# Block attention and two expert layers on one core: keys of the first block stored once and cut into windows by the matmul, with a new hand-written start order

## The chip, the cores and the metric

The program runs on one core of a Trainium2 chip. The metric is device time in microseconds (us) of one execution. The engines named here are TensorE (PE, with its weight loads shown apart as PEld), VectorE (DVE), ScalarE (ACT), GpSimd (POOL) and the queue that issues the transfers (SP). Each engine works through its own list in order and waits where an operand is not ready.

## The reference

Three layers follow each other on 4 x 768 tokens with 8 heads of 64 dimensions. The first is attention in chunks of 32 queries: each chunk sees 8 memory keys, 16 keys to its left, its own 32 and 8 to its right, so 64 keys in all.

```
for c in range(nc):                      # chunks of 32
    k_ctx = k[:, :, max(0, 32c-16) : min(S, 32c+40)]
    k_full = concat([mem_k, k_ctx])      # 8 + 56 keys
    a = softmax(q_c @ k_full.T / 8)
    out[:, :, chunk c] = a @ v_full
x = out as (3072 tokens, 512)
x = (s * relu(x @ w_in)**2 + b) @ w_out              # 512 -> 2048 -> 512
logits = x @ phi; slots = softmax over tokens of logits, transposed, @ x
slot_out = relu(slots @ w1[e]) @ w2[e]               # 8 experts, 4 slots each
result = softmax over slots of logits, @ slot_out
```

## The kernel before

The 3072 tokens are six blocks of 512 (16 chunks). A unit `u` of attention is one block and one pair of heads, so a block has four units; units 0 to 3 are the first block. For a unit, `Q[u % 2]` holds the queries of 16 chunks spread so that the two heads of a chunk stand in 64 columns, with zeros where the other head's dimensions are. The keys lie in memory as 16 windows of 64 (8 memory keys and 56 of context), overlapping ones written out twice, and `load_k` brings all of a unit, 512 KB, in one transfer. `att_qk` (L198) makes 16 products, one a chunk: 64 weight columns (the queries) against 64 moving columns (the window). An fp32 product is two instructions in the trace, so a unit shows 32. Even and odd pairs of chunks write the upper and lower 64 partitions of a bank.

Then `att_exp` takes the maximum over each window (L212), subtracts it (L213) and lets ACT exponentiate (L214). `att_norm` sums (L218), adds a tiny number (L219), inverts (L220), and POOL multiplies (L221). `att_tr` transposes on PE (L227) and copies the result into `PB[u % 2]` in two halves: the first on ACT (L236), the second on ACT (L238, argument `fast`) or on DVE (L240). `att_pv` multiplies with the values (L247) and ACT and DVE split the result into a high and a low part (L251, L263).

The second layer's weights come as halves of a packed form in seven staging slots (`w_load`). A half is decoded by `w_begin` (L293 on DVE, L294 and L295 on ACT) and `w_end` (L301 on DVE). `wi_high` (L312) and `wi_low` (L316) split a decoded half. `mm_h` (L332) and `mm_job` (L353) are the large products of the second layer, which follow for the rest of the kernel.

The first block's order is a string written by hand, `START`. Each token is a step and the number is its unit: `q`, `k`, `v`, `w`, `c` issue transfers (queries, keys, values, a weight half, the constants), `z` runs warming products on PE (L927), `S` spreads the queries (L184 on ACT, L185 on POOL or DVE), `A` is `att_qk`, `m` `att_exp`, `n` `att_norm`, `T` `att_tr`, `P` `att_pv`, `x` the low part, `D` and `E` the decoding, `I` and `i` the split of a weight, `H` a quarter of the first `mm_h`. The string fixes the order on every engine and queue; after it a scheduler mixes in the DVE and ACT work of the next steps. Eight transfers can be under way, and the ninth is issued when the first has landed.

Of the kernel before, what the change touches and what calls it, by code (L numbers as in the profile page):

```python
# [15 lines left out]
P = 128  # L16
NB = 6
NF = 16
NHP = 4
CB = 16  # L20
# [3 lines left out]
NEG = -3.0e38  # L24
EPS = 1e-9
START = (
# [3 lines left out]
)  # L30
# [8 lines left out]
def tile_attention_moe_softmoe(  # L39
    ctx: ExitStack,  # L40
    tc: tile.TileContext,
    q0d: bass.AP,
    qd: bass.AP,
    kd: bass.AP,
# [104 lines left out]
    def qv(u):  # L149
        return Q[u % 2].rearrange("p (c h n) -> p c h n", h=2, c=CB)  # L150
# [4 lines left out]
    def kv(u):  # L155
        t = K[u] if u < 2 else (Y[u - 2] if u < 4 else K[u % 2])
        return t.rearrange("p (c n) -> p c n", c=CB)

# [19 lines left out]
    def load_k(u):  # L178
        j, hp = jh(u)
        sp.dma_start(out=kv(u), in_=kd[j, hp].rearrange("p (c n) -> p c n", c=CB))  # L180

# [9 lines left out]
    def att_qk(u, b):  # L191
        S = b.rearrange("p (t n) -> p t n", t=8)
        qt, kt = qv(u), kv(u)
        for i in range(4):
            for z in range(2):
                for par in range(2):
                    c = 4 * i + 2 * par + z
                    pe.matmul(S[64 * par:64 * par + 64, 2 * i + z, :], lhsT=qt[:, c].rearrange("p h n -> p (h n)"), rhs=kt[:, c, :],  # L198
                              start=True, stop=True)

# [712 lines left out]
    with tc.manual_schedule(engines={mybir.EngineType.PE, mybir.EngineType.SP}):  # L913
# [30 lines left out]
        def s_pv(u):  # L944
# [4 lines left out]
        steps = {  # L949
            "c": lambda _: sp.dma_start(out=cons, in_=cd),  # L950
            "q": load_q,
# [7 lines left out]
            "n": lambda u: att_norm(u, pool),  # L959
            "T": lambda u: att_tr(u, sbank(), u < 3),  # L960
            "P": s_pv,
# [278 lines left out]
def _layouts(q, k, v, mem_k, mem_v, moe_w_in, moe_w_out, moe_s, moe_b, moe2_phi, moe2_w1, moe2_w2):  # L1240
# [21 lines left out]
    vw = windows(v, mem_v)  # L1262
    kt = np.ascontiguousarray(kw.transpose(0, 2, 3, 5, 1, 4)).reshape(NB, NHP, P, CB * 64)
    vt = np.ascontiguousarray(
# [15 lines left out]
    for d0, width in PARTS:  # L1280
        per = 1024 // width
        w2.append(moe2_w2[:, :, d0:d0 + width].reshape(2, 4, 8 // per, per, P, width)
                  .transpose(0, 2, 1, 4, 3, 5).reshape(-1, P, 1024))
    return {"q0d": np.ascontiguousarray(qt[0]), "qd": qp, "kd": kt, "vd": vt, "wd": w.view(np.int64), "e1d": np.ascontiguousarray(moe2_w1),
            "e2d": np.concatenate(w2), "cd": c}
# [15 lines left out]
```

## Time and profile before

| what | value |
|---|---|
| median of 3 runs | 672.23 us (671.5 to 672.26) |
| the profiled execution | 673.84 us, of which 672.0 us lie from its first to its last instruction |
| PE busy | 653.4 us, 97% of the span |
| DVE, ACT busy | 397.1 us, 328.3 us |
| TensorE clock granted, mean | 0.993 of full |

Start times in the trace count from the span's first instruction. A busy PE counts a matmul's whole passage, and the passages of neighbours overlap, so the time from one start to the next is shorter than the duration of one.

### The profile page before, as it was taken

Reading aid. Unit: us, or ns where it says so; the run is one execution under the profiler, and the core shown is the slowest. Engines: PE = TensorE matmul, PEld = TensorE weight load, DVE = VectorE, ACT = ScalarE, POOL = GpSimd, SP = SyncE. Lnnn points to the kernel's source line nnn. Section 1 sums busy time; section 2 is a strip of 40 time slices with the busy share of each in tenths; the row PEclk is TensorE's granted clock in tenths of the full one; section 3 lists DMA queues with packets and bytes.
Section 4 is the critical chain, followed back from the end, with each engine's and each line's share of the span. In section 5 each row is a group of like instructions: output and inputs, shape, how many; then the busy total and the mean of one; then the engine's idle time right before and its main releaser. Section 6 shows DMA issues by size and latency. Waiting matters only on the chain.

```text
span 672.0 us, 12487 instructions
## 1 busy us (share of the span) xinstructions
PE 653.4 (97%) x4983; PEld 518.7 (77%) x4983; DVE 397.1 (59%) x707; ACT 328.3 (49%) x592; POOL 123.3 (18%) x118
## 2 busy tenths in 40 slices
PE   7899999999999998999999999999999999999995
PEld 4678888888878887888788887887887888877374
DVE  4799997666774577655576576434444445333333
ACT  4898884554654455444445554233442334233332
POOL 5100000233433585344434100000000000000000
PEclk9999999999999998999999999999999999999999
DMA  8999934476556856788754684256777777999987
GB/s 337 407 398 360 322 115 161 152 224 202 204 176 191 296 206 246 269 297 297 263 209 173 220 305 134 93 180 233 249 258 250 272 248 279 409 362 409 346 328 283
DMA packets 50745, 174.09 MB, mean 259 GB/s; under 512 B 5632, under 2 KB 5632, under 8 KB 50688
## 3 DMA queue, kind: packets, MB, share of 16 engines
q1 hardware_dynamic: 50688, 173.30, 72.0%
q8 instruction: 39, 0.64, 0.4%
q14 instruction: 18, 0.15, 0.1%
HBM read 139.72 MB, written 33.55 MB: 258 GB/s over the span
## 4 chain that ended last, share of the span: by engine, by line
PE 92%; DVE 4%; ACT 2%; issue 1%; DVEq 0%; POOL 0%; ACTq 0%; POOLq 0%
PE bank L353 39%; PE bank L671 22%; PE bank L332 11%; PE bank L247 4%; PE bank L198 4%; PE bank L1163 2%; PE bank L1122 2%; PE bank L227 2%; PE bank L405 2%; PE bank L379 1%; PE bank L421 1%; PE bank L1192 1%; PE bank L927 1%; DVE w L301 0%; ACT sp L295 0%
## 5 line engine op out<-in xcount | busy, mean ns | idle before, releaser
L353 PE MATMUL bank<-g,wo 128*128 128x512 f32 x672 | 165.0, 395 | 0.0
L353 PEld LDWEIGHTS bank<-g,wo 128*128 128x128 f32 x672 | 123.6, 188 | 28.7 <-issue 1.7
L332 PE MATMUL bank<-x,wi 128*128 128x512 f32 x384 | 93.1, 390 | 0.2 <-DVE x L263 0.2
L332 PEld LDWEIGHTS bank<-x,wi 128*128 128x128 f32 x384 | 71.8, 188 | 15.5 <-DVE x L263 0.6
L686 ACT ACTIVATE rt1n<-y1n 128x1024 f32<-128x1024 f32 x16 | 16.9, 1059 | 73.3 <-DVE y1n L797 73.3
L1090 POOL MEMSET x10n<- 128x1024 f32 x1 | 1.0, 957 | 241.1 <-ACT ees L413 241.1
L341 DVE SCALAR_TENSOR_TENSOR rt<-bank,cons,rt 128x512 f32<-128x512 f32 x32 | 23.9, 747 | 33.8 <-ACT rt L336 33.7
L316 POOL TENSOR_TENSOR wi<-w,wi 128x512 fp32r<-128x512 f32 x16 | 20.7, 1292 | 116.9 <-ACT wi L312 110.9
L792 DVE TENSOR_TENSOR y1n<-bank,y1n 128x512 f32<-128x512 f32 x16 | 11.1, 691 | 45.7 <-PE bank L671 45.6
L679 ACT ACTIVATE g<-rt0n,cons 128x512 fp32r<-128x512 f32 x32 | 23.1, 723 | 20.2 <-DVE rt0n L689 20.2
L324 ACT ACTIVATE wo<-w 128x512 fp32r<-128x512 f32 x32 | 20.1, 629 | 24.7 <-PE bank L353 16.0
L325 POOL TENSOR_TENSOR wo<-w,wo 128x512 fp32r<-128x512 f32 x16 | 22.3, 1397 | 50.0 <-ACT wo L324 37.7
L312 ACT ACTIVATE wi<-w 128x512 fp32r<-128x512 f32 x32 | 20.1, 627 | 23.0 <-PE bank L332 21.9
L683 DVE SCALAR_TENSOR_TENSOR g<-rt0n,cons,g 128x512 fp32r<-128x512 f32 x32 | 24.7, 773 | 10.0 <-ACT g L679 9.5
L353 PE MATMUL bank<-g,yt0n 128*128 128x512 f32 x120 | 30.1, 398 | 0.2 <-DVE sp L372 0.2
L353 PE MATMUL bank<-g,yt1n 128*128 128x512 f32 x120 | 29.6, 395 | 0.0
L247 PEld LDWEIGHTS bank<-pb,v 128*64 128x64 f32 x704 | 22.6, 139 | 8.9 <-issue 3.5
L343 DVE SCALAR_TENSOR_TENSOR g<-rt,cons,g 128x512 fp32r<-128x512 f32 x32 | 24.1, 754 | 5.4 <-ACT g L342 4.9
L689 DVE SCALAR_TENSOR_TENSOR rt0n<-bank,cons,rt0n 128x512 f32<-128x512 f32 x16 | 12.0, 750 | 25.8 <-ACT rt0n L686 25.8
L198 PEld LDWEIGHTS bank<-k,q 128*64 128x64 f32 x704 | 23.2, 142 | 5.1 <-issue 4.7
L342 ACT ACTIVATE g<-rt,cons 128x512 fp32r<-128x512 f32 x32 | 23.0, 720 | 7.2 <-DVE rt L341 7.1
L353 PEld LDWEIGHTS bank<-g,yt0n 128*128 128x128 f32 x120 | 21.9, 188 | 5.8 <-DVE sp L372 0.9
(484 smaller groups left out, 1461.2 us busy)
## 6 DMA issues: line engine op xcount, KB each, us to landing
sp<-wd SPq DMA_DIRECT2D x24, 512.0 KB, 9.8
wo<-dws SPq DMA_DIRECT2D x24, 512.0 KB, 4.5
k<-kd SPq DMA_DIRECT2D x22, 512.0 KB, 7.0
v<-vd SPq DMA_DIRECT2D x22, 512.0 KB, 5.3
q<-qd SPq DMA_DIRECT2D x20, 512.0 KB, 6.6
dws<-wo SPq DMA_DIRECT2D x16, 512.0 KB, 6.9
yt0n<-dws SPq DMA_DIRECT2D x12, 512.0 KB, 4.9
yt1n<-dws SPq DMA_DIRECT2D x12, 512.0 KB, 4.2
```

The costliest lines, as they stand in the source:

```text
L198: pe.matmul(S[64 * par:64 * par + 64, 2 * i + z, :], lhsT=qt[:, c].rearrange("p h n -> p (h n)"), rhs=kt[:, c, :], start=True, stop=True)
L247: pe.matmul(b[64 * h:64 * h + 64, 64 * m:64 * m + 64], lhsT=vt[:, m, h, :], rhs=pb[:, m // 2, m % 2, h].rearrange("p z n -> p (z n)"), sta ...
L316: (dve if n < NF else pool).tensor_tensor(out=r32(t[:, 1]), in0=raw, in1=t[:, 0], op=ALU.subtract)
L325: (dve if n < NF else pool).tensor_tensor(out=r32(t[:, 1]), in0=raw, in1=t[:, 0], op=ALU.subtract)
L332: pe.matmul(HB[n % 2], lhsT=r32(w[:, a, kt, :]), rhs=r32(x[:, b]), start=(kt == 0 and i == 0), stop=(kt == 3 and i == 2))
L341: dve.scalar_tensor_tensor(out=t, in0=HB[n % 2], scalar=s_col, in1=r, op0=ALU.mult, op1=ALU.mult)
L342: act.activation(out=r32(g[:, 0]), in_=t, func=AF.Identity, bias=b_col)
L343: dve.scalar_tensor_tensor(out=r32(g[:, 1]), in0=t, scalar=b_col, in1=g[:, 0], op0=ALU.add, op1=ALU.subtract)
L353: pe.matmul(yb[dt], lhsT=r32(w[:, a, dt * 128:dt * 128 + 128]), rhs=r32(g[:, b]), start=(first and i == 0), stop=(last and i == 2))
L671: pe.matmul(b, lhsT=r32(wv[:, a, kt, :]), rhs=r32(xv[:, c]), start=(first and kt == 0 and i == 0), stop=(kt == 1 and i == 2), skip_group_c ...
L679: act.activation(out=r32(hl(dst)[:, 0]), in_=t, func=AF.Identity, bias=b_col)
L683: dve.scalar_tensor_tensor(out=r32(g[:, 1]), in0=t, scalar=b_col, in1=g[:, 0], op0=ALU.add, op1=ALU.subtract)
```

## The change

Keys of the first block are stored once per head pair: `KRAW` = 536 columns (16 empty ones, then the block's 512 positions and the 8 behind it) and the 8 memory keys, so 544 columns, 272 KB where 512 KB were. The windows of a chunk are cut by the matmul: `att_qk` makes two products a chunk for the units 0 to 3, one of 56 moving columns out of the context and one of 8 moving columns out of the memory keys, both with the same queries as weights. Other blocks keep their windows. The constants come in two loads: the identity (128 columns) early, the rest behind `q4`. The first weight half is issued behind `k3`, no longer ahead of the constants. The start order is a new one, and only units 0 and 1 copy both halves of the transposed weights on ACT (before: 0 to 2).

```diff
+KRAW = 16 + 512 + 8
 START = (
-    "q0 k0 q1 k1 w1 c0 q2 k2 v0 q3 k3 v1 w1 v2 w1 v3 w1 "
-    "z2 S0 A0 z1 S1 A1 m0 n0 D0 S2 m1 A2 E0 T0 I0 n1 S3 m2 z1 P0 T1 A3 i0 n2 x0 m3 P1 T2 D1 n3 x1 E1 H0 P2 "
-    "k4 w1 q4 w1 k5 v4 w1 q5 T3 H1 P3 x2 D2 H2 x3 E2 D3 E3 y0 w9 v5"
+    "q0 k0 q1 k1 c0 q2 k2 v0 q3 k3 w1 v1 w1 v2 w1 v3 w1 "
+    "z2 S0 A0 z1 S1 A1 m0 S2 A2 m1 n0 S3 A3 m2 n1 T0 D0 m3 n2 P0 E0 T1 n3 I0 x0 T2 i0 P1 D1 H0 x1 T3 P2 E1 "
+    "k4 w1 q4 c1 w1 k5 v4 w1 q5 x2 H1 P3 D2 H2 x3 E2 D3 E3 y0 w9 v5"
 )
 def load_k(u):
     j, hp = jh(u)
-    sp.dma_start(out=kv(u), in_=kd[j, hp].rearrange("p (c n) -> p c n", c=CB))
+    if j:
+        sp.dma_start(out=kv(u), in_=kd[j - 1, hp].rearrange("p (c n) -> p c n", c=CB))
+    else:
+        sp.dma_start(out=kraw(u), in_=k0d[hp])
 def att_qk(u, b):
...
-                    pe.matmul(S[64 * par:64 * par + 64, 2 * i + z, :], lhsT=qt[:, c].rearrange("p h n -> p (h n)"), rhs=kt[:, c, :],
-                              start=True, stop=True)
+                    dst, q = S[64 * par:64 * par + 64, 2 * i + z, :], qt[:, c].rearrange("p h n -> p (h n)")
+                    if u < NHP:
+                        kt = kraw(u)
+                        pe.matmul(dst[:, 8:64], lhsT=q, rhs=kt[:, 32 * c:32 * c + 56], start=True, stop=True)
+                        pe.matmul(dst[:, 0:8], lhsT=q, rhs=kt[:, KRAW:KRAW + 8], start=True, stop=True)
+                    else:
+                        pe.matmul(dst, lhsT=q, rhs=kv(u)[:, c, :], start=True, stop=True)
 steps = {
-            "c": lambda _: sp.dma_start(out=cons, in_=cd),
+            "c": lambda i: sp.dma_start(out=cons[:, (0, 128)[i]:(128, 516)[i]], in_=cd[:, (0, 128)[i]:(128, 516)[i]]),
...
-            "T": lambda u: att_tr(u, sbank(), u < 3),
+            "T": lambda u: att_tr(u, sbank(), u < 2),
```

PE's list at the start, before, from unit 0's scores (`k_101` and `q_99`) to unit 2's transposes (L227 on `rt_97`):

```order
L198 MATMUL bank_176<-k_101,q_99 64x64 x16
L927 MATMUL bank_180<-w_82 128x512
L198 MATMUL bank_177<-k_102,q_100 64x64 x16
L198 MATMUL bank_178<-y_109,q_99 64x64 x16
L227 MATMUL bank_181<-cons,ep 128x128 x4
L927 MATMUL bank_180<-w_82 128x512
L247 MATMUL bank_182<-pb_105,v_103 64x64 x16
L227 MATMUL bank_175<-cons,ep 128x128 x4
L198 MATMUL bank_176<-y_110,q_100 64x64 x16
L247 MATMUL bank_177<-pb_106,v_104 64x64 x16
L227 MATMUL bank_178<-cons,rt_97 128x128 x4
```

PE's list with the change, from the last pair of unit 3's scores (`y_110` and `q_100`) on:

```order
L208 MATMUL bank_181<-y_110,q_100 64x56
L209 MATMUL bank_181<-y_110,q_100 64x8
L239 MATMUL bank_182<-cons,ep 128x128 x4
L259 MATMUL bank_175<-pb_105,v_103 64x64 x16
L239 MATMUL bank_176<-cons,ep 128x128 x4
L239 MATMUL bank_177<-cons,rt_97 128x128 x4
L259 MATMUL bank_178<-pb_106,v_104 64x64 x16
L344 MATMUL bank_179<-x_87,wi_83 128x512 x3
L239 MATMUL bank_181<-cons,rt_97 128x128 x4
L259 MATMUL bank_182<-pb_105,yt_107 64x64 x16
L344 MATMUL bank_179<-x_88,wi_83 128x512 x3
L259 MATMUL bank_175<-pb_106,yt_108 64x64 x16
```

Each unit of the first block now has 16 such pairs (L208 and L209), and the scores of unit 3 have moved ahead of the first transposes. The warming products ahead of units 0 and 1 stand as before; the one ahead of unit 0's values is gone.

POOL's list, before, from the spreading of unit 1's queries (L185) through the multiplications of the four units (L221):

```order
L185 COPY q_100<-rt_98 64x16x32
L221 ISA
L221 TENSOR_TENSOR ep<-ep,ast_171 128x512
L185 COPY q_99<-w_81 64x16x32
L221 TENSOR_TENSOR ep<-ep,ast_172 128x512
L185 COPY q_100<-w_81 64x16x32
L221 TENSOR_TENSOR rt_97<-rt_97,ast_171 128x512
L221 TENSOR_TENSOR rt_97<-rt_97,ast_172 128x512
```

The same stretch of POOL's list with the change:

```order
L192 COPY q_100<-rt_98 64x16x32
L192 COPY q_99<-w_81 64x16x32
L233 ISA
L233 TENSOR_TENSOR ep<-ep,ast_171 128x512
L192 COPY q_100<-w_81 64x16x32
L233 TENSOR_TENSOR ep<-ep,ast_172 128x512
L233 TENSOR_TENSOR rt_97<-rt_97,ast_171 128x512
L233 TENSOR_TENSOR rt_97<-rt_97,ast_172 128x512
```

Both late spreads moved up by one place: unit 2's stands ahead of the first multiplication, unit 3's between the first and the second.

ACT's list, before, from the first copies of transposed weights (`pb_105` of unit 0) on:

```order
L236 ACTIVATE pb_105<-bank_181 64x16x32
L238 ACTIVATE pb_105<-bank_181 64x16x32
L312 ACTIVATE wi_83<-w_67 128x512
L184 ACTIVATE q_100<-w_81 64x16x32
L214 ACTIVATE rt_97<-rt_97 128x512
L251 ACTIVATE x_87<-bank_182 128x512
L236 ACTIVATE pb_106<-bank_175 64x16x32
L238 ACTIVATE pb_106<-bank_175 64x16x32
L214 ACTIVATE rt_97<-rt_97 128x512
L251 ACTIVATE x_88<-bank_177 128x512
```

ACT's list with the change from the same copies on:

```order
L248 ACTIVATE pb_105<-bank_182 64x16x32
L250 ACTIVATE pb_105<-bank_182 64x16x32
L306 ACTIVATE sp_112<-sp_112 128x512
L307 ACTIVATE sp_112<-sp_112 128x512
L226 ACTIVATE rt_97<-rt_97 128x512
L263 ACTIVATE x_87<-bank_175 128x512
L248 ACTIVATE pb_106<-bank_176 64x16x32
L250 ACTIVATE pb_106<-bank_176 64x16x32
L324 ACTIVATE wi_83<-w_67 128x512
L248 ACTIVATE pb_105<-bank_177 64x16x32
```

The decoding of the first weight half (L306, L307; before L294, L295) moved from ahead of unit 2's spread to behind the first copies; the spread of unit 3 and the exponential of unit 2 moved ahead of them.

## Rows read from the trace of the kernel before

**Rows 1.** Busy time of each engine in four stretches, with granted clock, transfer share and GB/s
```profile
core 0: us, PE busy (x) PEld busy (x) DVE busy (x) ACT busy (x) POOL busy (x), PEclk, DMA share, GB/s
0.00:30.00 30.00, 22.67 (x292) 15.32 (x293) 18.16 (x40) 17.89 (x30) 10.99 (x20) 0.94 0.94 367
30.00:46.00 16.00, 15.14 (x93) 12.03 (x92) 15.85 (x32) 15.47 (x29) 0.00 (x0) 1.00 1.02 397
46.00:100.00 54.00, 53.77 (x404) 44.44 (x405) 53.26 (x103) 47.93 (x86) 0.00 (x0) 1.00 0.78 278
100.00:600.00 500.00, 497.75 (x3286) 403.73 (x3285) 286.26 (x474) 224.99 (x397) 111.36 (x97) 1.00 0.67 234
```

**Rows 2.** Timeline of PE from 0 to 52 us: start, duration, instruction, idle before
```profile
1.31 3.78 PE L927 MATMUL bank<-w 128*128 128x512 f32 x4 [1.31 <-POOL w L923]
5.13 1.98 PE L198 MATMUL bank<-k,q 128*64 128x64 f32 x32
7.04 1.13 PE L927 MATMUL bank<-w 128*128 128x512 f32 x2
8.27 1.15 PE L198 MATMUL bank<-k,q 128*64 128x64 f32 x32
12.69 1.15 PE L198 MATMUL bank<-y,q 128*64 128x64 f32 x32 [3.27 <-ACT q L184]
13.77 1.09 PE L227 MATMUL bank<-cons,ep 128*128 128x128 f32 x4
29.48 3.47 PE L332 MATMUL bank<-x,wi 128*128 128x512 f32 x14 [0.25 <-DVE x L263]
46.23 0.66 PE L227 MATMUL bank<-cons,ep 128*128 128x128 f32 x4 [1.09 <-DVE ep L221]
```

**Rows 3.** Transfers issued at 1.18, 2.12 and 15.28 us: size, time to landing
```profile
k<-kd SPq DMA_DIRECT2D x1, 512.0 KB, 3.8
...
k<-kd SPq DMA_DIRECT2D x1, 512.0 KB, 6.0
...
sp<-wd SPq DMA_DIRECT2D x1, 512.0 KB, 11.3
```

**Rows 4.** Weight loads of 32, 64, 128 columns, and PE around 619 us
```profile
L1072 PEld LDWEIGHTS bank<-dmat,acc x32: 106/113/113, 620.2 to 620.5; 128*32 128x32 f32 x32
L198 PEld LDWEIGHTS bank<-y,q x64: 133/138/138, 12.7 to 19.4; 128*64 128x64 f32 x64
L353 PEld LDWEIGHTS bank<-g,wo x672: 186/188/192, 34.0 to 614.6; 128*128 128x128 f32 x168
L1092 PE MATMUL bank<-one,mxr x8: 165/176/186, 619.1 to 619.2; 1*32 1x1 f32 x8
619.13 0.24 PE L1092 MATMUL bank<-one,mxr 1*32 1x1 f32 x8
```

**Rows 5.** Groups of instructions from 5 to 46 us: busy, mean ns, idle before
```profile
L212 DVE TENSOR_REDUCE ast<-bank 128x8 f32<-128x512 f32 x5 | 3.5, 692 | 0.2
L220 DVE RECIPROCAL ast<-ast 128x8 f32<-128x8 f32 x5 | 1.0, 202 | 0.1
L221 POOL TENSOR_TENSOR ep<-ep,ast 128x512 f32<-128x512 f32 x2 | 2.1, 1042 | 6.2 <-DVE ast L220 4.2 <-DVE bank L209 2.0
L185 POOL COPY q<-w 64x512 f32<-64x512 f32 x2 | 1.2, 608 | 0.1
L236 ACT ACTIVATE pb<-bank 64x512 f32<-64x512 f32 x4 | 2.4, 588 | 1.8 <-PE bank L227 1.8
L240 DVE COPY pb<-bank 64x512 f32<-64x512 f32 x1 | 0.7, 695 | 0.5 <-ACT pb L236 0.5
L295 ACT ACTIVATE sp<-sp 128x512 uint32<-128x512 uint8 x11 | 7.2, 667 | 0.0
```

**Rows 6.** PE in four stretches: busy, granted clock, transfer share, GB/s
```profile
7.00:10.50 3.50, 2.31 (x36) 1.00 0.96 368
10.50:13.90 3.40, 1.21 (x33) 0.99 1.04 418
13.90:17.30 3.40, 3.40 (x22) 0.51 1.02 405
```

More of the change, by code (lines that the diff above doesn't have):

```diff
@@ L42, in tile_attention_moe_softmoe @@
     q0d: bass.AP,
+    k0d: bass.AP,
     qd: bass.AP,
@@ L155, in kv, with kraw @@
     def kv(u):
-        t = K[u] if u < 2 else (Y[u - 2] if u < 4 else K[u % 2])
-        return t.rearrange("p (c n) -> p c n", c=CB)
+        return K[u % 2].rearrange("p (c n) -> p c n", c=CB)
+    def kraw(u):
+        return (K[u] if u < 2 else Y[u - 2])[:, 0:KRAW + 8]
     def vv(u):
@@ L192, in att_qk @@
         S = b.rearrange("p (t n) -> p t n", t=8)
-        qt, kt = qv(u), kv(u)
+        qt = qv(u)
         for i in range(4):
@@ L1262, in _layouts @@
     vw = windows(v, mem_v)
-    kt = np.ascontiguousarray(kw.transpose(0, 2, 3, 5, 1, 4)).reshape(NB, NHP, P, CB * 64)
+    kt = np.ascontiguousarray(kw[1:].transpose(0, 2, 3, 5, 1, 4)).reshape(NB - 1, NHP, P, CB * 64)
+    k0 = np.zeros((NHP, 2, D, KRAW + 8), f)
+    k0[:, :, :, 16:KRAW] = k[0, :, 0:KRAW - 16].reshape(NHP, 2, KRAW - 16, D).transpose(0, 1, 3, 2)
+    k0[:, :, :, KRAW:] = mem_k[0].reshape(NHP, 2, 8, D).transpose(0, 1, 3, 2)
+    k0 = k0.reshape(NHP, P, KRAW + 8)
     vt = np.ascontiguousarray(
@@ L1283, in _layouts @@
                   .transpose(0, 2, 1, 4, 3, 5).reshape(-1, P, 1024))
-    return {"q0d": np.ascontiguousarray(qt[0]), "qd": qp, "kd": kt, "vd": vt, "wd": w.view(np.int64), "e1d": np.ascontiguousarray(moe2_w1),
+    return {"q0d": np.ascontiguousarray(qt[0]), "k0d": k0, "qd": qp, "kd": kt, "vd": vt, "wd": w.view(np.int64), "e1d": np.ascontiguousarray(moe2_w1),
             "e2d": np.concatenate(w2), "cd": c}
```

## The prediction, made before the change was run

> **What bounds the kernel now.** I read the busy times of four stretches first [rows 1]. From 46 us on PE is busy 53.77 of 54 us and then 497.75 of 500, so whatever delays PE's arrival at 46 us is paid in full at the end, and whatever brings it forward is gained in full, unless a later wait takes it. In the first 30 us PE shows 22.67 us busy, much of it warming products, and DVE and ACT stand idle for about 12 us each; the transfers are at 0.94 of their engines. From 30 to 46 us DVE (15.85 of 16) and ACT (15.47) are full with decoding weights, and PE is full but for one wait: at 46.23 the transposes of unit 4 had waited 1.09 us for DVE's `ep` [rows 2]. So the change, which touches only the first stage, counts by two things: when the last quarter of the first large product (L332, 29.48 us [rows 2]) can start, and how much of DVE's and ACT's list is done by then.
>
> Then I read the timeline of PE in the first stage and the landings beside it. The first key transfer was issued at 1.18 us and landed 3.8 us later, at 4.98; the second landed at 2.12 + 6.0 = 8.12 [rows 3]. The scores of units 0 and 1 started at 5.13 and 8.27 [rows 2], so both started just behind their keys, though unit 0's also just behind the warming products (1.31 + 3.78 = 5.09). Unit 2's scores came only at 12.69, after a wait of 3.27 us for the spread on ACT.
>
> **The keys.** Each of the four transfers shrinks from 512 to 272 KB, together 983 KB; with 198 KB of constants moved back and a weight half issued later, unit 1's keys have some 4.1 quarter megabytes ahead of and in them instead of 6. Between the landings at 4.98 and 8.12 lay three quarter megabytes, so they land near 6 us, an estimate. Unit 0's scores can start when the warming products let go: four of them in 3.78 us are 0.9 apart, so at about 4.9 instead of 5.13. That is all that the loads give to unit 0. Unit 1's keys stop being the limit; the warming product ahead of it is next.
>
> **The scores.** This is the term that decides. A unit had 32 instructions and gets 64: the second set has 8 moving columns but loads the same 64 weight columns. What does such an instruction cost? At the later pace 32 of them took 12.69 to 13.77, so 0.034 us from start to start; in unit 0 they took 5.13 to 7.04, so 0.060 [rows 2]. Two column halves of the array work side by side, so an instruction holds its half 0.067 us. The trace has no load of 64 columns with 8 moving ones. Bound from below: they cost only their moving columns, an eighth, 32 x 0.034 / 8 = 0.14 us a unit. From above: an instruction of either kind costs the same, 1.08 us a unit. The weight load decides between them. Its recorded time grows from 0.113 us at 32 columns to 0.138 at 64 and 0.188 at 128 [rows 4], about 0.8 ns a column, so 64 columns take some 0.05 us, as long as the moving half of the product. The nearest row with hardly any moving work is L1092: 8 products of one column with 32-column loads in four quarters of the array. All 8 took 0.24 us of which one passage is 0.176 [rows 4], so two in a quarter start 0.04 apart, though a column should pass in about a nanosecond. That row says that the load sets the pace. I take the upper end, 64 x 0.034 = 2.2 us for a unit, and keep the lower for the range.
>
> The Trainium skill would price them otherwise: "TensorE: Matmul & The Clock Gate", section "Back-to-back issue gap", gives one floor of about 25 ns from start to start for any product up to 64 columns. By it a unit would take 64 x 0.025 = 1.6 us, and the sum below would be some 0.9 us instead of 2.1. The trace differs already for 64 columns: 34 ns with the load.
>
> **The chain to the first transposes.** Unit 0: at the slow pace until about 7.04, so 36 of 64, then 28 x 0.034; last start near 8.0. The warming product behind it takes 1.13 [rows 2] less the overlap, so unit 1's scores start at 9.05 (before 8.27) and are complete at 9.05 + 2.2 + 0.2 = 11.4 (before 9.42). DVE then takes unit 1's maximum and difference and only after them unit 0's sum: 1.5 + 1.1 us by the 0.69 and 0.20 of [rows 5], to 14.0. POOL multiplies (0.18 from DVE to POOL, 1.04), to 15.25, and only then spreads unit 3's queries (0.61), because that copy stands behind the multiplication in POOL's list. Unit 3's scores run 15.95 to 18.1, and unit 0's transposes stand behind them in PE's list: 18.1 instead of 13.77 [rows 2]. Of these 4.3 us the pairs give 3 x 1.05; the order gives the rest.
>
> **From there to the large product.** Much that lay behind the transposes is already done then: all scores, the spreads, three of the four differences. ACT has ten rows from the transposes' end (18.8) to the first half of unit 2's copy, some 0.58 from start to start by the 0.59 and 0.67 of [rows 5], whose ends overlap: 24.6. The second half now is DVE's (one L240 of 0.70, moved from ACT) and, as before in the trace, it waits for ACT's first half; 25.3. DVE's low part of the first weight split, 0.65; PE's first quarter 0.7, unit 3's transposes 0.66, unit 2's values 1.1: 28.4. ACT's high part, decode and split, 1.8; DVE's low part, a decode's end and the last low part, 2.0: the last quarter starts at 32.2 against 29.48, +2.7.
>
> By then DVE has one decoding row (L301) more behind it than before had at that point, worth 0.6, and ACT has more than one. So DVE, which is full from here on, is 2.1 us late and hands over `ep` of unit 4 at about 46.2 + 2.1 = 48.3. PE itself needs 15.7 us from the last quarter to that wait (29.48 to 45.14), 47.9, so the wait shrinks to 0.4 but does not vanish. PE reaches its full stretch 2.1 us late. The constants' second part and the later weight halves lie off this path: the decoder L295 had no idle time at all before it from 5 to 46 us [rows 5].
>
> **The sum.** +2.1 us on a span of 672.0. The profiled execution lasted 673.84 and the runs' median is 672.23; I add the difference to the median: 674.3 us. What a measurement of this kernel can tell from no change is 0.2%, 1.3 us.
>
> **Rivals.** (1) *The lower clock.* In 10.5 to 13.9 us PE was busy 1.21 of 3.40 us, and in the next stretch the granted clock was 0.51 [rows 6], half of 2.4 GHz, where it had been 1.00 after a stretch with 2.31. With the change PE is idle from the end of unit 2's scores (13.4) to 15.95, so the same can fall on unit 3's scores and the first transposes: the latter took 1.09 there instead of 0.66, and half of unit 3's scores would take twice their time, 0.6. Together +1.0: 675.3. Before paid for it too, but in a spot with slack. (2) *The pairs are cheap.* If the 8-column products cost their columns alone, unit 1 and the transposes come 0.9 us a unit earlier, 2.8 in all; then ACT waits for the weight half that before issued at 15.28 and that landed 11.3 us later [rows 3], by my count at 23 to 24 us now, and gives half of it back. The sum is -0.7 to +0.7, 671.5 to 673: no change that can be told. The 25 ns floor that the Trainium skill gives in "TensorE: Matmul & The Clock Gate", section "Back-to-back issue gap", would end near the upper end of this too. (3) *Faster: the loads end the first stage.* If what really holds the stage is the stream, everything behind the keys comes 983 KB at 0.41 MB a us earlier, 2.4 us: 669.8. For it: 0.94 to 1.04 of the transfer engines in the rows, and unit 1 starting 0.15 us behind its keys. Against it: L295 never waited. It decides once a unit's scores take less than about 1.4 us, for only then does the early start of units 2 and 3 fill DVE's idle 12 us. (4) *The halves of the array don't overlap* when four instructions in a row use one half: a unit then takes up to 3 us and the sum doubles, 677. L1092's four quarters did overlap, against it.
>
> **Chances.** Forecast 0.38; the lower clock on top 0.14; pairs cheap or their cost covered 0.29; loads end the stage 0.16; no overlap 0.03. So slower by over 0.2%: 0.55; within 0.2%: 0.29; faster: 0.16. The range reaches from the cheap pairs with part of the loads' gain, 670.8, to beyond the lower clock, 676.2; its forecast part alone is 673.6 to 675.5.
>
> **What would show it.** Right: a unit's scores at 12 to 20 us taking 2.1 to 2.3 us; unit 1 complete near 11.4; first transposes near 18; the last quarter of the first large product near 32; the wait at unit 4's transposes under 1 us. Wrong: scores under 1.5 us, which leads to rival 2 or 3; transposes before 16 us; or the large product on time although the transposes are late, which would say that the order behind them packs ACT and DVE better than I count.

## The result, and the profile after

| | before | with the change |
|---|---|---|
| median of nine runs each (range) | 672.23 us (671.5 to 675.5) | 677.44 us (675.84 to 680.36) |
| profiled execution, of it the span | 673.84, 672.0 us | 677.46, 675.7 us |
| mean granted clock | 0.993 | 0.989 |

The ratio to the kernel before is 1.0059, with a 95% interval from 1.0043 to 1.0075: 4.0 us slower (2.9 to 5.0). The medians lie further apart, 5.2 us, because the runs of either kernel form groups some 1.6 us apart, and the median falls into the lower group before and into the higher one with the change. The sign and the place were as predicted; the size was not. The forecast was +2.1 us, 674.3. A rise of 4.0 us on 672.23 is 676.2, the very upper end of the range, and the median itself lies 1.2 us above it.

The busy times of the four stretches with the change, to be held against [rows 1]:

```profile
core 0: us, PE busy (x) PEld busy (x) DVE busy (x) ACT busy (x) POOL busy (x), PEclk, DMA share, GB/s
0.00:30.00 30.00, 23.97 (x380) 18.47 (x380) 15.49 (x35) 15.01 (x25) 11.00 (x20) 0.83 0.96 363
30.00:46.00 16.00, 15.09 (x117) 11.73 (x117) 15.61 (x31) 15.26 (x28) 0.00 (x0) 1.00 0.73 247
46.00:100.00 54.00, 52.97 (x346) 43.44 (x346) 52.85 (x103) 47.48 (x85) 0.00 (x0) 1.00 0.78 297
100.00:600.00 500.00, 497.77 (x3341) 403.86 (x3340) 288.87 (x479) 227.80 (x401) 111.32 (x97) 1.00 0.67 233
```

From 100 to 600 us nothing has changed (497.77 of 500). In the first 30 us DVE did 15.49 us of work where it had done 18.16, and ACT 15.01 where it had done 17.89: both come out of the first stage with nearly 3 us of their lists undone. And the granted clock of that stretch fell from 0.94 to 0.83.

PE's timeline with the change, the places of [rows 2]: the warming product, the first products of unit 2's scores, unit 3's scores, the first transposes, the values of units 0 and 1, the last quarter of the first large product, unit 4's transposes, and the product behind a wait near 260 us:

```profile
7.17 1.12 PE L939 MATMUL bank<-w 128*128 128x512 f32 x2
10.12 0.34 PE L208 MATMUL bank<-y,q 128*64 128x56 f32 x4
10.25 0.28 PE L209 MATMUL bank<-y,q 128*64 128x8 f32 x4
10.35 0.34 PE L208 MATMUL bank<-y,q 128*64 128x56 f32 x4
14.86 0.34 PE L208 MATMUL bank<-y,q 128*64 128x56 f32 x4 [2.69 <-POOL q L192]
17.80 1.12 PE L239 MATMUL bank<-cons,ep 128*128 128x128 f32 x4
20.21 1.98 PE L259 MATMUL bank<-pb,v 128*64 128x64 f32 x32 [1.30 <-ACT pb L250]
24.53 1.75 PE L259 MATMUL bank<-pb,v 128*64 128x64 f32 x32 [0.44 <-ACT pb L250]
33.68 3.51 PE L344 MATMUL bank<-x,wi 128*128 128x512 f32 x14 [0.65 <-DVE x L275]
50.40 0.66 PE L239 MATMUL bank<-cons,ep 128*128 128x128 f32 x4 [1.03 <-DVE ep L233]
263.60 0.97 PE L683 MATMUL bank<-w0n,wi0n 128*128 128x512 f32 x3 [2.07 <-DVE rt0n L701]
```

The first transposes start at 17.80 (13.77 before), the last quarter at 33.68 (29.48) and unit 4's transposes at 50.40 (46.23). So 4.0 us are lost by the first transposes, and all of it is still there at 263.60, where the same product stood at 259.43 before. The granted clock by stretch (third number from the end; columns as in the first block above), the continuation of [rows 6]:

```profile
7.00:10.50 3.50, 3.50 (x88) 2.72 (x87) 1.56 (x5) 1.24 (x3) 0.71 (x2) 1.00 1.04 403
10.50:13.90 3.40, 1.67 (x57) 1.58 (x55) 3.23 (x8) 1.15 (x2) 0.81 (x1) 1.00 1.02 384
13.90:17.30 3.40, 2.44 (x58) 2.44 (x59) 1.80 (x5) 0.63 (x1) 1.88 (x3) 0.76 1.02 417
17.30:20.70 3.40, 2.10 (x26) 1.68 (x24) 2.42 (x6) 1.70 (x3) 0.06 (x1) 0.50 1.02 404
20.70:24.10 3.40, 3.39 (x36) 2.87 (x34) 2.31 (x5) 2.63 (x6) 1.67 (x2) 0.50 1.03 408
24.10:27.50 3.40, 2.68 (x35) 2.18 (x36) 1.71 (x3) 2.76 (x5) 0.36 (x1) 0.74 1.02 406
```

Behind PE's idle stretch from 12.2 to 14.86 the clock went to half (1.2 GHz) in the midst of unit 3's scores, and it came back only in the last of these stretches. Summed over the four (a stretch at 0.76 is at half for 0.48 of its length) that is 10.2 us at half clock; before it was 3.4. In it fall the transposes of three units and the values of units 0 and 1: 1.98 and 1.75 us, where a unit's values take 1.15 at full clock.

### The profile page after: what moved, and what is told of

Its sections match the earlier page's. It is cut to its first block, busy times and chain, and to the rows that moved or that the text cites. A ratio compares the mean times of both kernels' runs of the same rounds, so it can differ in the third digit from the quotient of the medians.

```text
span 675.7 us, 12745 instructions
## 1 busy us (share of the span) xinstructions
PE 657.8 (97%) x5109; PEld 524.0 (78%) x5109; DVE 397.9 (59%) x708; ACT 328.3 (49%) x591; POOL 123.3 (18%) x118
## 4 chain that ended last, share of the span: by engine, by line
PE 93%; DVE 4%; ACT 2%; issue 1%; POOL 0%; DVEq 0%; POOLq 0%
PE bank L365 39%; PE bank L683 22%; PE bank L344 12%; PE bank L259 3%; PE bank L211 3%; PE bank L1175 2%; PE bank L1134 2%; PE bank L239 2%; PE bank L417 2%; PE bank L391 1%; PE bank L433 1%; PE bank L1204 1%; PE bank L939 1%; PE bank L208 1%; PE bank L471 0%
## 5 line engine op out<-in xcount | busy, mean ns | idle before, releaser
L328 POOL TENSOR_TENSOR wi<-w,wi 128x512 fp32r<-128x512 f32 x16 | 21.0, 1314 | 119.7 <-ACT wi L324 113.7
L259 PE MATMUL bank<-pb,v 128*64 128x64 f32 x704 | 26.8, 232 | 1.7 <-ACT pb L250 1.7
L355 DVE SCALAR_TENSOR_TENSOR g<-rt,cons,g 128x512 fp32r<-128x512 f32 x32 | 24.1, 754 | 5.4 <-ACT g L354 4.9
```

What stands on the lines that cost most here:

```text
L259: pe.matmul(b[64 * h:64 * h + 64, 64 * m:64 * m + 64], lhsT=vt[:, m, h, :], rhs=pb[:, m // 2, m % 2, h].rearrange("p z n -> p (z n)"), sta ...
L328: (dve if n < NF else pool).tensor_tensor(out=r32(t[:, 1]), in0=raw, in1=t[:, 0], op=ALU.subtract)
L355: dve.scalar_tensor_tensor(out=r32(g[:, 1]), in0=t, scalar=b_col, in1=g[:, 0], op0=ALU.add, op1=ALU.subtract)
```

## The experiments

Each kernel was profiled once and timed against the kernel before. Marks in the table, all from PE's timeline, in us: T, first transposes; Q, last quarter of the first large product; U, unit 4's transposes; M, the product behind the wait near 260 us; and the time at half clock before 28 us.

| run | T | Q | U | M | half | ratio (95%) |
|---|---|---|---|---|---|---|
| before | 13.77 | 29.48 | 46.23 | 259.43 | 3.4 | 1 |
| the change | 17.80 | 33.68 | 50.40 | 263.60 | 10.2 | 1.0059 (1.0043 to 1.0075) |
| e1, old order | 18.19 | 35.91 | 52.84 | 266.03 | 10.2 | 1.0085 (1.0066 to 1.0104) |
| e2, windows, new order | 15.75 | 30.18 | 46.55 | 259.74 | 3.4 | 1.0014 (1.0000 to 1.0028) |
| e3, one product | 14.80 | 30.24 | 47.73 | 260.93 | 13.7 | 1.0012 (0.9997 to 1.0026) |
| e4, clock held | 16.86 | 30.84 | 47.18 | 260.40 | 0 | 1.0028 (1.0004 to 1.0052) |
| e5, pairs alone | 16.43 | 33.51 | 50.74 | 263.93 | 6.8 | 1.0076 (1.0060 to 1.0092) |
| e6, e2 with clock held | 16.02 | 30.31 | 46.64 | 259.86 | 0 | 0.9998 (0.9986 to 1.0010) |
| e7, e3 with clock held | 14.59 | 28.59 | 44.94 | 258.14 | 0 | 0.9978 (0.9966 to 0.9991) |
| e8, before with clock held | 13.39 | 28.54 | 44.94 | 259.02 | 0 | 0.9987 (0.9974 to 1.0001) |
| e9, first gap alone | 17.28 | 31.27 | 47.61 | 260.80 | 0 | 1.0012 (0.9999 to 1.0025) |
| e11, spread first | 16.70 | 30.68 | 47.48 | 260.68 | 0 | 1.0039 (1.0014 to 1.0065) |
| e12, e11 with warming | 17.16 | 31.10 | 48.38 | 261.57 | 0 | 1.0050 (1.0032 to 1.0068) |
| e10, before, two gaps | 13.24 | 28.38 | 44.78 | 258.84 | 0 | 0.9995 (0.9981 to 1.0008) |

From M to the end the spans are alike but for one thing: a lapse of the clock behind the wait near 260, which is there in some executions only (412.0 to 412.6 us from M to the end with it, 410.7 to 411.0 without, e10 apart). It parts the runs of a kernel into groups some 1.6 us apart, so M and U say more than a single span. The marks are those of one execution, and two things in them differ between executions. The first is the pace at the start: unit 0's scores begin at about half the later pace, and the pace doubles at 5.3 us with the change and in e4, near 6.6 in e11 and only behind unit 0's scores in the kernel before. In e9 the warming product ahead of unit 1 starts for that reason at 7.60 instead of 7.17, 0.43 us later. The second is the time at half clock, which the mean granted clock of each run shows. Where a product is added on PE, the scheduler also gives DVE and ACT a slightly different list from Q on; differences at U of a few tenths are read only where the row that makes them is named.

**e1: the old order with the small keys.**

```diff
-    "z2 S0 A0 z1 S1 A1 m0 S2 A2 m1 n0 S3 A3 m2 n1 T0 D0 ...
+    "z2 S0 A0 z1 S1 A1 m0 n0 D0 S2 m1 A2 E0 T0 I0 n1 S3 ...
...
-            "T": lambda u: att_tr(u, sbank(), u < 2),
+            "T": lambda u: att_tr(u, sbank(), u < 3),
```

> The change with its keys, loads and pairs of products, but the compute order of the kernel before (and three units copied on ACT). Theory 1, that pairs and new order together push the first transposes back: they come near 14.7 us (13.8 before, 17.8 with the change) and the time is about 1 us above before, ratio 1.001 to 1.002. Rival, the order alone: ratio within 0.001 of 1. Rival, the pairs alone: most of the 4 us stays, ratio 1.004 or more.

It was the slowest of all, U at 52.84. It is no clean test: in the old order DVE decodes the first weight half ahead of unit 1's maximum, and in the new loads that half comes behind the keys. DVE's timeline of e1 shows the wait:

```profile
12.24 0.58 DVE L305 TENSOR_SCALAR sp<-sp 128x512 f32<-128x512 f32 x1 [1.59 <-DMA sp<-wd]
```

Order and loads of the change belong together; e5 was made to part them from the pairs.

**e2: windows of 512 KB and one product a chunk, with the new order and loads.**

```diff
-    "q0 k0 q1 k1 w1 c0 q2 k2 v0 q3 k3 v1 w1 v2 w1 v3 w1 "
-    "z2 S0 A0 z1 S1 A1 m0 n0 D0 S2 m1 A2 E0 T0 I0 n1 ...
+    "q0 k0 q1 k1 c0 q2 k2 v0 q3 k3 w1 v1 w1 v2 w1 v3 w1 "
+    "z2 S0 A0 z1 S1 A1 m0 S2 A2 m1 n0 S3 A3 m2 n1 T0 ...
...
```

> The kernel before with its windows of 512 KB and one product a chunk, but the new start order, the new order of the loads, the constants in two loads and two units copied on ACT. Theory 1: scores of units 0, 1 and 3 take 1.15 us each again, first transposes near 15.2 us (unit 1's keys land at 8.1 again), time 0 to 1.5 us above before, ratio 1.000 to 1.002. Rival, the order alone: transposes near 17 us or the product on time lost all the same, ratio 1.004 or more. Rival, the pairs alone: ratio below 1.000.

U at 46.55, 0.3 us behind the kernel before, although the first transposes came 2 us later. In this execution the order by itself costs next to nothing: what it puts ahead of the transposes is done by then. But it is the fastest of e2's twelve runs, with a mean granted clock of 0.996; seven of the others have 0.984 to 0.990, so the clock fell for longer in them. By all twelve the order costs 0.9 us (0 to 1.9).

**e3: one product of 64 columns a chunk on the small keys.** The memory keys are left out of the scores; 8 neighbouring columns stand in their place.

```diff
-                        pe.matmul(dst[:, 8:64], lhsT=q, rhs=kt[:, 32 * c:32 * c + 56], start=True, stop=True)
-                        pe.matmul(dst[:, 0:8], lhsT=q, rhs=kt[:, KRAW:KRAW + 8], start=True, stop=True)
+                    kt = kraw(u)[:, 32 * c:32 * c + 64] if u < NHP else kv(u)[:, c, :]
+                    pe.matmul(dst, lhsT=q, rhs=kt, start=True, stop=True)
```

> The change with one product of 64 adjacent raw keys a chunk in the first block: the memory keys are left out there and 8 neighbours stand in their place. So the second product alone is taken away. Theory 1: first transposes near 14.3 us, the half clock gone or shorter, last quarter of the first product near 29, time 0.5 to 1.5 us below before, ratio 0.998 to 0.9995. Rival, the order alone: ratio stays at 1.003 or more. Rival, the clock alone: ratio follows the granted clock after 15 us, not the transposes.

The transposes came 3.0 us earlier than with the change, but still 13.7 us passed at half clock, and U was 1.5 us behind the kernel before. Theory 1's transposes near 14.3 and last quarter near 29 were missed. The pairs are not what holds the clock down.

**e4: the change with warming products, two behind unit 2's scores, one behind the first transposes.**

```diff
-    ... S2 A2 m1 n0 S3 A3 m2 n1 T0 D0 ...
+    ... S2 A2 z2 m1 n0 S3 A3 m2 n1 T0 z1 D0 ...
```

> The change with two more warming products between the scores of units 2 and 3, and one between the first transposes and unit 0's values; nothing else. Theory of the clock: full clock from 14 to 26 us, transposes 0.66 for 1.12, values 1.15 for 1.98 and 1.75, about 1.5 to 2 us come back, ratio to before 1.003. If the clock cost nothing on the path: ratio stays 1.006.

PE's timeline of e4:

```profile
16.86 0.66 PE L239 MATMUL bank<-cons,ep 128*128 128x128 f32 x4
18.81 1.15 PE L259 MATMUL bank<-pb,v 128*64 128x64 f32 x32 [0.44 <-ACT pb L250]
30.84 3.48 PE L344 MATMUL bank<-x,wi 128*128 128x512 f32 x14 [0.56 <-DVE x L275]
47.18 0.66 PE L239 MATMUL bank<-cons,ep 128*128 128x128 f32 x4 [0.68 <-DVE ep L233]
```

The stretch of e4 in which the changed kernel stood at 0.50:

```profile
17.30:20.70 3.40, 2.81 (x40) 1.68 (x38) 2.79 (x6) 3.08 (x6) 0.99 (x1) 1.00 1.02 404
```

Work that computes nothing makes the kernel 3.2 us earlier at U (50.40 to 47.18). From the first transposes to the last quarter PE now needs 13.98 us, against 15.88 with the change. At the last quarter the lower clock is 2.84 of the change's 4.20 us (33.68 to 30.84). The other 0.4 at U comes from DVE's list: with the change a split row (L328 at 49.11) stands ahead of unit 4's `ep` (49.66), and in e4 behind it (47.05 and 46.45). By the runs alone, 1.0028 and 1.0059, the two are not told apart; e9 below is.

**e5: the pairs alone.** The kernel before, with only the small keys and the two products a chunk; loads, constants and order as before.

```diff
-            t = K[u] if u < 2 else (Y[u - 2] if u < 4 else K[u % 2])
...
-                    pe.matmul(S[64 * par:64 * par + 64, 2 * i + z, :], lhsT=qt[:, c].rearrange("p h n -> p (h n)"), rhs=kt[:, c, :],
-                              start=True, stop=True)
+                        pe.matmul(dst[:, 8:64], lhsT=q, rhs=kt[:, 32 * c:32 * c + 56], start=True, stop=True)
+                        pe.matmul(dst[:, 0:8], lhsT=q, rhs=kt[:, KRAW:KRAW + 8], start=True, stop=True)
```

> The kernel before with one part of the change: keys stored once and two products a chunk in units 0 to 3; loads, constants and start order as before. My theory (the pairs cost about 1 us a unit, the lower clock adds to it when PE's work thins out): unit 2's scores still start near 12.7 because ACT's spread sets them, take 2.1 us, first transposes at 15 us, unit 4's transposes at 47.0 to 47.8 (before 46.23), ratio 1.001 to 1.0025. If the old order together with the pairs is what makes the clock stay low (the earlier run with the old order had 10.2 us of it): unit 4's transposes at 49 us or later, ratio above 1.004. If the pairs are hidden in this order: unit 4's transposes within 0.3 us of 46.2 and a ratio of 1.000. In the earlier run of the old order the first weight half came behind the keys; if that alone made its +6.6 us, this run is near the first figure.

Unit 2's scores and the first transposes in PE's timeline of e5:

```profile
12.91 0.47 PE L208 MATMUL bank<-y,q 128*64 128x56 f32 x4 [2.54 <-ACT q L191]
16.43 1.12 PE L239 MATMUL bank<-cons,ep 128*128 128x128 f32 x4
50.74 0.66 PE L239 MATMUL bank<-cons,ep 128*128 128x128 f32 x4 [1.56 <-DVE ep L233]
```

My figure of 47.0 to 47.8 missed; the second figure came. The unit's 64 products fall wholly into the stretch at half clock and take 3.5 us, and half clock lasts 6.8 us instead of 3.4. So pairs and clock multiply each other: a longer piece of work in a slow stretch. The old order is no refuge: with the clock's part the pairs cost more in it (+4.5 against the kernel before) than in the new one (+3.9 against e2).

**e6: e2 with the warming products of e4.**

```diff
-    ... S2 A2 m1 n0 S3 A3 m2 n1 T0 D0 ...
+    ... S2 A2 z2 m1 n0 S3 A3 m2 n1 T0 z1 D0 ...
```

> The windows of before (one product a chunk, 512 KB a unit) in the new order, with two warming products behind unit 2's scores and one behind the first transposes. My theory (the clock's lapse in the first stage costs time in this order too): granted clock 1.00 from 7 to 30 us, unit 3's scores in 1.15 instead of 1.98 us, last quarter of the first large product at 29.3 to 29.8 (30.18 without the warming), unit 4's transposes at 45.3 to 46.0 (46.55 without), ratio 0.998 to 1.000. Rival (the lapse of 3.4 us in this order lies beside DVE's and ACT's work and costs nothing): unit 4's transposes at 46.4 to 46.7, ratio 1.001.

Undecided. U stayed at 46.64, but unit 1's keys landed late in this execution, as its row shows; in e2 the same scores started at 8.11. From there to the first transposes e6 needs 6.81 us and e2 7.64, so the held clock gave back 0.8 us that the later keys had taken. By the runs, 0.9998 and 1.0014, e6 and e2 are not told apart.

```profile
9.21 1.15 PE L198 MATMUL bank<-k,q 128*64 128x64 f32 x32 [1.05 <-DMA k<-kd]
```

**e7: e3 with the warming products of e4** (the memory keys again left out); against e3:

```diff
-    ... S2 A2 m1 n0 S3 A3 m2 n1 T0 D0 ...
+    ... S2 A2 z2 m1 n0 S3 A3 m2 n1 T0 z1 D0 ...
```

> The changed kernel with one product of 64 columns a chunk (the memory keys are left out, 8 neighbouring columns stand in their place) and the warming products of the run that held the clock. Told apart: what the second product costs when the clock is held. With pairs and the clock held, unit 4's transposes stood at 47.18 us. If the pairs are worth about 1 us a unit on the path, as my sum has it: first transposes at 14.0 to 14.6, last quarter at 28.5 to 29.5, unit 4's transposes at 45.0 to 46.0, ratio 0.997 to 1.000. If, with the clock held, the pairs are mostly covered by DVE and ACT: unit 4's transposes at 46.6 to 47.2, ratio 1.001 to 1.003, although the first transposes come 2 us earlier.

PE's timeline of e7:

```profile
7.77 1.15 PE L207 MATMUL bank<-k,q 128*64 128x64 f32 x32
14.59 0.66 PE L235 MATMUL bank<-cons,ep 128*128 128x128 f32 x4
28.59 3.48 PE L340 MATMUL bank<-x,wi 128*128 128x512 f32 x14 [0.57 <-DVE x L271]
44.94 0.66 PE L235 MATMUL bank<-cons,ep 128*128 128x128 f32 x4 [0.69 <-DVE ep L229]
```

With the clock held, one product instead of two is 2.27 us earlier at T, 2.25 at Q, 2.24 at U and 2.26 at M than in e4. That is the price of the pairs in these two executions, paid in full from end to end. It is rather too small: e7 ran unit 0's scores at the slow pace for longer (32 products in 1.76 us, 1.15 in e3), so that unit 1's came at 7.77 and not at e3's 7.16. With e3's start the price would be 2.9 us, an estimate. And e7 is 1.3 us ahead of the kernel before at M. That this is the small keys' doing is not shown, because e7 also holds the clock, as e8 does without them.

**e8: the kernel before with three warming products ahead of unit 2's scores.**

```diff
-    "z2 S0 A0 z1 S1 A1 m0 n0 D0 S2 m1 A2 ...
+    "z2 S0 A0 z1 S1 A1 z3 m0 n0 D0 S2 m1 A2 ...
```

> The kernel before with three warming products ahead of unit 2's scores, in the gap of 3.27 us in which PE waited for the spread. It measures what the lower clock cost before. If it lay in slack, as I assumed: granted clock 1.00 from 7 to 30 us, first transposes near 13.6, unit 4's transposes within 0.2 us of 46.2, ratio 0.9995 to 1.0005. If it cost what the longer one cost with the change (3.2 us for 10.2 us of it, so 0.3 us a us): 1.0 us earlier, 45.2, ratio 0.998 to 0.999.

PE's timeline of e8:

```profile
28.54 3.45 PE L332 MATMUL bank<-x,wi 128*128 128x512 f32 x14 [0.24 <-DVE x L263]
44.94 0.60 PE L227 MATMUL bank<-cons,ep 128*128 128x128 f32 x4
59.79 0.66 PE L227 MATMUL bank<-cons,ep 128*128 128x128 f32 x4 [0.76 <-DVE ep L221]
```

U came 1.3 us earlier, more than either figure; but the wait for DVE, gone there, is back at the next unit (0.76 us at 59.79), and at M 0.4 us of the gain is left. The kernel before lost little to its lower clock, as DVE's wait at the next unit suggests. At the last quarter and at U e8 stands where e7 does (28.54 and 28.59, 44.94 in both), with keys of 512 KB; at M e7 is 0.9 us ahead. By the runs e8 is 0.1% ahead of the kernel before, not told from no change.

**e9: the change with the warming products in the first gap alone.**

```diff
-    ... S2 A2 m1 n0 S3 A3 m2 n1 T0 D0 ...
+    ... S2 A2 z2 m1 n0 S3 A3 m2 n1 T0 D0 ...
```

> The changed kernel with two warming products between unit 2's and unit 3's scores alone (in the 2.7 us in which PE waits for POOL's spread), none behind the first transposes. If that one gap makes the whole lower stretch (10.2 us with the change): granted clock 1.00 up to 30 us, unit 4's transposes at 47.0 to 47.5, as with both warming products, ratio 1.002 to 1.003. If the clock also falls at the gap behind the first transposes: 3.4 us or more of half clock from about 17 to 24 us, last quarter of the first large product at 31.5 to 33, unit 4's transposes at 48 to 49.5, ratio 1.0035 to 1.005.

PE's timeline of e9, the warming product ahead of unit 1 and unit 4's transposes:

```profile
7.60 1.13 PE L939 MATMUL bank<-w 128*128 128x512 f32 x2
47.61 0.66 PE L239 MATMUL bank<-cons,ep 128*128 128x128 f32 x4 [0.66 <-DVE ep L233]
```

No half clock at all before 30 us, and U at 47.61. The gap between unit 2's and unit 3's scores alone set off the 10.2 us. The 0.43 us by which U lies behind e4's are there at 7.60 already (7.17 in e4), so the warming behind the first transposes was worth nothing. Here the runs tell as well: e9's ratio is at most 1.0025, the change's at least 1.0043.

**e11: the change with POOL's spread of unit 3 ahead of its multiplication of unit 0.**

```diff
-    ... S2 A2 m1 n0 S3 A3 m2 n1 ...
+    ... S2 A2 m1 S3 n0 A3 m2 n1 ...
```

> The changed kernel with one step moved: POOL's spread of unit 3 ahead of its multiplication of unit 0, so that unit 3's scores need not wait for that multiplication. If the order on POOL makes both the late transposes and the low clock, as my steps have it: unit 3's scores behind unit 2's at 12.1 to 12.5 (14.86 with the change), at full clock in 2.1 us, first transposes at 14.7 to 15.3 (17.80), no half clock before 15 us and at most 3.4 us of it after, last quarter of the first large product at 30 to 31.5, unit 4's transposes at 46.6 to 48.0, ratio 1.001 to 1.003. If the pairs themselves keep the clock down: half clock for 7 us or more all the same, unit 4's transposes at 49 or later, ratio above 1.005.

Unit 3's scores and the following marks in PE's timeline of e11:

```profile
13.73 0.34 PE L208 MATMUL bank<-y,q 128*64 128x56 f32 x4 [1.00 <-issue]
15.38 0.22 PE L209 MATMUL bank<-y,q 128*64 128x8 f32 x1 [0.81 <-issue]
16.70 0.66 PE L239 MATMUL bank<-cons,ep 128*128 128x128 f32 x4
47.48 0.66 PE L239 MATMUL bank<-cons,ep 128*128 128x128 f32 x4 [1.15 <-DVE ep L233]
```

The same stretch of the clock in e11:

```profile
17.30:20.70 3.40, 1.85 (x38) 1.49 (x37) 2.78 (x6) 3.24 (x6) 1.04 (x1) 1.00 1.03 407
```

In the profiled execution the clock held without any warming, with all pairs in place, and U came 2.9 us earlier than with the change. The first transposes missed their figure (16.70, not 15): ACT's half of the same spread ran only at 13.02, behind the exponential that waits for unit 1's maximum, and in the scores PE stood 0.81 us for nothing that the profile shows. So POOL's order makes the long gap, and the gap the low clock. It does not hold in every execution: the profiled one has a mean granted clock of 0.998, three others have 0.990 and 0.991. Three of its twelve runs lie at 680.1 us, which widens its ratio so far that by the runs alone e11 is not told apart from the change (one of nine with the change, two of twelve of e4 and one of ten of e12 lie there too, none of the kernel before, and none was seen in a trace). The lower clock does not explain them, for their mean granted clock is 0.996 to 0.998. The profiled execution took 673.19.

**e12: e11 with one warming product behind unit 3's scores and one behind the first transposes.** Against e11:

```diff
-    ... S3 n0 A3 m2 n1 T0 D0 ...
+    ... S3 n0 A3 z1 m2 n1 T0 z1 D0 ...
```

> As the run with the spread moved, with one warming product behind unit 3's scores and one behind the first transposes. If the clock is then held and the pairs' remaining price is their 1 us a unit for the units on the path: first transposes at 15.0 to 15.8, last quarter at 29.3 to 30.3, unit 4's transposes at 45.6 to 46.6, ratio 0.998 to 1.001. If DVE's and ACT's lists set the end whatever PE does: unit 4's transposes at 47.0 to 47.4 as in the run with both warming products in the order of the change, ratio 1.002 to 1.003.

A miss: U at 48.38, 0.9 us behind e11, with a wait of 1.61 us for DVE. The clock held already, so the products only delayed the transposes (17.16 against 16.70), and DVE's list came out another.

**e10: e8, and three warming products in the wait near 260 us.**

```diff
                 att_turn(4 * NHP + p + 1, D)
+                if p == 0:
+                    for _ in range(3):
+                        pe.matmul(C, lhsT=cons[:, 0:128], rhs=cons[:, 0:512], start=True, stop=True)
```

> The kernel before with warming products in the two places where its clock was seen to fall: three ahead of unit 2's scores, and three in the wait of 2.06 us near 259 us (on a bank that is free there). If the lower clock behind that wait is what parts the runs into two groups 1.6 us apart: granted clock 1.00 from 258 to 268 us, all runs in one group at 670.8 to 671.8, ratio 0.996 to 0.998. If the groups have another cause: runs at 673 to 673.5 remain among them and the ratio stays at 0.9985 to 1.000.

PE's timeline of e10, near 260 us and near the end:

```profile
256.60 2.74 PE L842 MATMUL bank<-cons 128*128 128x512 f32 x6
258.84 1.21 PE L671 MATMUL bank<-w0n,wi0n 128*128 128x512 f32 x3
608.03 5.69 PE L353 MATMUL bank<-g,wo 128*128 128x512 f32 x24 [0.46 <-DMA wo<-dws]
```

The clock stayed at 1.00 there, and in all twelve runs the mean granted clock is 0.997 to 0.999. The runs no longer form two groups 1.6 us apart but spread over 671.7 to 673.3. By its figures the second expectation came all the same: three runs lie at 673.0 to 673.3, and the ratio is 0.9995. So the lapse is not all that moves the runs. In the profiled execution 0.46 us went into a wait for a weight transfer at 608 us that neither the kernel before nor e8 shows; the rest stays open. Of the kernels here only e7, which leaves the memory keys out, is told apart as faster than the kernel before.

## Why the prediction was right and wrong

**Where it holds.** PE is full from 46 us on and what comes late there is paid in full: 4.17 us at U, 4.17 at M. Unit 0's scores gained next to nothing from the smaller transfer (5.02 against 5.13). POOL's copy behind the multiplication made unit 3's scores wait (2.69 us on L192, starts at 14.86; I had said 15.95). Unit 1's keys landed at 7.1 us (2.11 + 5.0) and not near 6. The 983 KB of the prediction are thousands of bytes; in the KB of the rows it is 4 times 240, so 960.

**Luck at the first transposes.** They came at 17.80 against 18.1 as worked out, but by two errors that cancel. Unit 3's scores started 1.1 us earlier than worked out, since unit 0's left the slow pace at 5.3 us and not at 7.04 and the pairs were cheaper; and then they took 2.94 us instead of 2.15, because the clock fell in their midst. With the clock held (e4) the transposes, the last quarter and U stand at 16.86, 30.84 and 47.18, where I had 18.1, 32.2 and 48.3. So the sum without the clock was 1.1 to 1.4 us too long, which hid part of what the clock cost.

**The pairs, a little too dear.** In a full-speed stretch eight instructions, four of each kind, take 0.23 us (10.12 to 10.35 us): 0.13 from the first of four with 56 moving columns to the first of four with 8, and 0.10 from there to the next four. Over unit 2's scores that is 0.034 each for those with 56 columns, as I took it from 32 products of before, and 0.024 each for those with 8. So an instruction of either kind did not cost the same, as my upper end had it; the one with 8 columns cost 0.7 of the other, still far above the eighth of my lower end. A unit takes 1.9 us, not 2.2. The Trainium skill, "TensorE: Matmul & The Clock Gate", section "Back-to-back issue gap", states a floor of about 25 ns from start to start for products of up to 64 columns. The products with 8 columns stand at it in this trace, those with 56 at 34 ns. On the path the pairs came to 2.26 us (e4 against e7), 2.9 with like starts, where my sum had three units by 1.05.

**The step that failed: the lower clock.** I had the mechanism and its place, as rival 1 ("PE is idle from the end of unit 2's scores (13.4) to 15.95, so the same can fall on unit 3's scores and the first transposes"), but with 0.14 of the chance and a price of +1.0, as if it would end where the stretch of before did. It lasted 10.2 us and took in two units' values and three units' transposes too. By its own marks the sum went so: the first transposes 0.3 us earlier than predicted; from them to the last quarter 15.88 us where I had 14.1, +1.8; from there to U 16.72 us where I had 16.1, +0.6; together 2.1 us, the whole difference between the predicted 48.3 and the measured 50.40. That the +1.8 is the clock is shown by e4 and e9, where the same stretch took 13.98 and 13.99 us, and by e11, which removed the gap without adding work and took 13.98. The whole price, with what the clock took from unit 3's scores, is 2.8 us at the last quarter: 2.84 by e4, and by e9 2.41 plus the 0.43 of its later start. That is nearly three times the +1.0 of my rival.

**A credit that was spent again.** The +0.6 is as large as the decoding row that I had credited to DVE ("one decoding row more behind it, worth 0.6"). The credit was there: by the last quarter three such rows were done with the change (at 21.45, 30.06 and 32.34 us), two before (12.26 and 24.94). But the kernel before took 16.75 us from there to U and the change 16.72, since the split row of 0.64 us went ahead of unit 4's `ep` (L328 at 49.11; before, L316 behind it at 46.09). Where it stands behind, in e4 and e9, the stretch took 16.34. DVE's timeline with the change, the third decoding row and the end ahead of U:

```profile
32.34 0.68 DVE L313 SCALAR_TENSOR_TENSOR w<-sp 128x512 uint32<-128x512 uint32 x1
49.11 0.64 DVE L328 TENSOR_TENSOR wi<-w,wi 128x512 fp32r<-128x512 f32 x1
49.66 0.68 DVE L233 TENSOR_TENSOR ep<-ep,ast 128x512 f32<-128x512 f32 x1
```

**The rivals.** Pairs cheap (2) falls with the 0.024 us: 32 of them are 0.8 us a unit, not 0.14. Loads end the stage (3) falls as a forecast, and its gain is not told apart. With one product and the clock held M is 1.3 us ahead of the kernel before, but e8, with the large keys, is 0.4 ahead of it too. Against e6, which has the large keys in the same order, e7 is 1.7 us ahead; unit 1's scores start at 7.77 instead of 9.21 there, and some 1.1 us of that is e6's late landing (8.11 in e2). No overlap (4) is refuted by unit 2's scores: 64 instructions in 1.9 us.

So at M, in the executions that were profiled, e7 with small keys, new order and held clock stands 1.3 us ahead of the kernel before; the pairs take 2.26 us (e4), and the change without the warming another 3.2, of which 2.8 are the lower clock and 0.4 the place of DVE's row. How the 1.3 divides between keys, order and clock is not shown.

**Open.** Why half clock lasted 3.4 us in the kernel before and in e2, but 6.8 to 13.7 us in e5, the change and e3, behind gaps of the same size, was not settled. It is not fixed by the kernel: the mean granted clock goes from 0.984 to 0.997 over the runs of e2, from 0.985 to 0.996 over those of e3 and from 0.986 to 0.998 over those of the change. Nor is it settled where the runs at 680 us come from.

## What to carry to other kernels

When a transfer is made smaller by cutting its windows in the matmul, count the instructions and not the moving columns: one with 8 columns cost 0.7 of one with 56, and 128 more instructions cost 2.3 us or more on the path, while no run showed as large a gain by the 960 KB less to load. When an edit moves a step behind a wait of PE, price the clock behind that wait over all that follows until it is seen to return, not over the one product that follows, and try the same list with the waiting step's input first: here one copy moved ahead of one multiplication gave back 2.9 us at unit 4 without any added work, in the execution that was profiled. And read the marks of one execution beside the clock of all runs, for the profiled one can be the fastest of twelve.

## What the runs showed of the hardware that was not expected

- The clock stayed at half while PE was busy: 3.39 of 3.40 us between 20.7 and 24.1 us with the change, at 0.50. In e11 it stayed at 1.00 with PE busy 1.85 of 3.40. Before it fell PE had stood idle for 2.54 us in e5, 2.68 in e3, 2.69 in e2 and in the change, 3.27 in the kernel before; behind e11's waits of 1.00 and 0.81 us it did not fall.
- The wait of 2.06 us near 260 us is in every trace but e10's, and the lapse behind it only in some executions; it costs some 1.6 us.
- With a weight load of 64 columns for each instruction, products with 8 moving columns started 0.024 us apart and those with 56 0.034 apart at full clock.
- PE starts at about half its later pace (0.060 us from start to start in unit 0's scores of the kernel before, 0.034 later), and the time at which the pace doubles differs between executions, from 5.3 us with the change to about 7 in the kernel before. The profile's granted clock is 1.00 from 0 to 7 us in both.
- Unit 3's scores in e11 stood 0.81 us in their midst with nothing in the profile to wait for, and 0.54 us at the same place in e12.
